# A fused attention and mixture-of-experts kernel: scaling moved to ScalarE, one gather moved ahead, seven products for layer 1 of the last expert, smaller buffers

## The chip, the cores and the metric

One NeuronCore of a Trainium2 chip runs the whole program. The metric is the time of one execution on the device in microseconds (us), as the median of the runs; smaller is better. The engines are called TensorE (PE in the profile, its weight loads PEld), VectorE (DVE), ScalarE (ACT), GpSimd (POOL) and SyncE (SP). SP issues most of the DMA transfers.

## The reference

The first stage is causal attention in a window of 128 tokens with a distance bias per head. Its output, 4608 tokens x 512, is the input x of a mixture of eight experts whose gates P are balanced by eight rounds of row and column normalisation.

```python
def _attn_ref(q, k, v):                      # q, k, v: 8 x 8 x 576 x 64
    scores = scale * np.matmul(q, k.transpose(0, 1, 3, 2))
    ...
    scores = np.where(mask, scores + bias[None], -1000000000.0)
    ...
    return np.matmul(attn, v).astype(np.float32)

def _moe_ref(x, w_gate, w1, w2):             # N, D, E, F = 4608, 512, 8, 1024
    logits = x @ w_gate
    logits = logits - logits.max()
    P = np.exp(logits)
    for _ in range(8):
        P /= P.sum(1, keepdims=True) + 1e-09
        P /= P.sum(0, keepdims=True) + 1e-09
        P *= N / E
    out = np.zeros((N, D), dtype=np.float32)
    for e in range(E):
        h = np.maximum(x @ w1[e], 0.0)
        ye = h @ w2[e]
        out += P[:, e:e + 1] * ye
    return out.astype(np.float32)
```

## The kernel before

The order of each engine's work is the order in which the program issues it; nothing reorders it. The program has two stages.

In the first stage (up to about 341 us) attention is computed, and the experts 0 and 1 of the mixture are woven into it as filler, by a planner (`Filler`) that knows the cost of each piece. Their outputs, not yet scaled by the gates, go to memory (`ysp`), as does x (`xd`). Between the stages the gates P are computed (L814 to L852).

The second stage, which the change touches, computes the experts 2 to 7. The tokens stand in 18 groups of 256 (two blocks, m = 0 and 1, of 128). A unit is one group and one expert; there are 108 units, group by group, experts 2 to 7 within each. Iteration n of the main loop (L1094) does layer 1 of unit n and layer 2 of unit n-1, with their matmuls interleaved on TensorE.

Since a gate is positive, it may be applied to x before layer 1. So each unit scales its tokens by its expert's gate: `scale_x` (L883, two instructions of 128x512 on VectorE, L889, from the token tile `xtok` to a tile `xs`), and `turn_xs` (L897) transposes the two into `xset[n % 2]` with two DMA transposes that SP issues (L901). Scaling and transposing are done two units ahead. There are four `xs` tiles, two for each parity of n. After the scaling for expert 7, `load_x` fetches the next group's tokens into `xtok`.

Layer 1 has two forms. The plain one (`l1_bank`, L939) does four banks of eight matmuls with 256 moving columns, and ACT applies the relu to each bank (L957). The other form, used from unit 6 on for all experts but 7 (`strassen(n)`, L876), is the product of 2x2 blocked matrices in seven block products in place of eight. It needs four sums of the blocks of W1 (`quads_w1`, L917, once per expert, on VectorE, L929), four sums of the blocks of x (`sums_x`, L909, three instructions on VectorE, L913 to L915), and combines the products while they accumulate in three PSUM banks pa, pb and pc: ACT copies a bank into another so that two results can grow from a common part (L1114, L1123), puts one part into SBUF (`s5s`, L1118, alternating between two halves by n), and VectorE adds that part to pb and pc (L1128, L1132). Each product is `part` (L963): eight matmuls with 128 moving columns. ACT applies the relus (L981): slots 0, 3, 1 and 2 of `h[n]`, in this order. The order of a unit is written out by hand (L1108 to L1142): a11, s1, s2, a12, s3, s4, a22 name the W1 operands of the seven products in the order of issue.

Layer 2 is in the seven product form for all units. `make_sums` (L983) forms the sums of h on VectorE (L985 to L987), the first thing in the iteration after. `product(n-1, m)` (L996, L1005) accumulates product m in one half of a PSUM bank, over all the six experts of a group; the group's first expert starts it afresh. When a group ends, `gather` (L1028, L1047) adds the products to `acc` on VectorE: products 3, 4, 5 and 2 in the next group's first unit (expert 2), 6, 7 and 1 in its second (expert 3). In that second unit products 6 and 7 are gathered right after `make_sums`, the scaling follows, then the sums out of PSUM L1128 and L1132, and product 1 is gathered behind them (L1135). Then `finish` (L1049) writes `acc` out, and `load_y` (L1014) brings the group's outputs of experts 0 and 1 back; `begin` (L1018) adds them, scaled by their gates, to `acc`: block 0 in the unit of expert 5, block 1 in that of expert 6 (two VectorE instructions each, L1020 and L1023).

The tiles come from pools of tags with a fixed number of buffers: "xT" (4: two `xset`, `acc`, `y`), "yo" (6: four `xs` and two `xtok`), "xTt" (1: `s5s`), "pmm" (4 PSUM banks: pa, pb, pc of the running unit and the one after). A tile that reuses a buffer waits for the readers of the tile before. In the last group, layer 2 of expert 7 is not done in seven products but plainly (`plain`, L1061), behind the loop.

Of the kernel before, what the change touches and what calls it, by code (L numbers as in the profile page):

```python
# [9 lines left out]
FP16 = mybir.dt.float16  # L10
FP32 = mybir.dt.float32
# [3 lines left out]
def kernel(  # L15
# [10 lines left out]
    nc = tc.nc  # L26
    AF = mybir.ActivationFunctionType
    ALU = mybir.AluOpType
# [3 lines left out]
    HD = H * Dh  # L32
# [3 lines left out]
    P = 128  # L36
# [192 lines left out]
    if True:  # L229
# [642 lines left out]
        y = per.tile([P, 2, 2, HD], FP16, name="y", tag="xT", bufs=4)  # L872
        xtok = [acc.rearrange("p m d -> p (m d)").bitcast(FP16)[:, HD * i : HD * i + HD] for i in range(2)]
        xs = [xset[i // 2][:, 4 + 2 * (i % 2) : 6 + 2 * (i % 2), :].rearrange("p q n -> p (q n)") for i in range(4)]

        def strassen(n):  # L876
            return n >= E - 2 and units[n][1] < E - 1

        def load_x(g):
            for m in range(2):  # L880
# [2 lines left out]
        def scale_x(n):  # L883
            if n >= N:
                return
            g, e = units[n]
            for m in range(2):
                blk = 2 * g + m
                nc.vector.tensor_scalar(  # L889
                    out=xs[2 * (n % 2) + m], in0=xtok[m], scalar1=P_sb[:, blk, e : e + 1], scalar2=None, op0=ALU.mult  # L890
                )
# [70 lines left out]

        def part(n, ps, w, x, start=False):  # L963

            e = units[n][1]
            for j in range(NF2):
                for k in range(2):
                    nc.tensor.matmul(  # L968
                        out=ps[:, j, :],
                        lhsT=SL[e][w][:, k, P * j : P * j + P],  # L970
                        rhs=xset[n % 2][:, x, P * k : P * k + P],
                        start=(start and j == 0 and k == 0),
                        stop=(k == 1),
                        skip_group_check=True,
                    )
# [4 lines left out]
        def relu(n, slot, src):  # L980
            nc.scalar.activation(out=h[n][:, slot], in_=src, func=AF.Relu)  # L981
# [36 lines left out]
        def begin(g, m):  # L1018
            blk = 2 * g + m
            nc.vector.tensor_scalar(  # L1020
                out=acc[:, m, :], in0=y[:, 0, m, :], scalar1=P_sb[:, blk, 0:1], scalar2=None, op0=ALU.mult
            )
            nc.vector.scalar_tensor_tensor(  # L1023
                out=acc[:, m, :], in0=y[:, 1, m, :], scalar=P_sb[:, blk, 1:2], in1=acc[:, m, :],
                op0=ALU.mult, op1=ALU.add,
            )

        def gather(g, *which):  # L1028
            q4 = acc.rearrange("p m (c n) -> p (m c) n", c=2)
# [57 lines left out]
        load_last(E - 1)  # L1087
        w2f = per.tile([P, 4, NF2, HB], FP16, name="w2f", tag="w1t", bufs=2)
        todo += sums_of(6, F1_6, w2f[:, 2], w2f[:, 3]) + sums_of(7, aux[:, 0], w2f[:, 0], w2f[:, 1])
        s5s = per.tile([P, 2, NF2, P], FP32, name="s5s", tag="xTt", bufs=1)  # L1090
        turn_xs(1)
        xs[:] = [per.tile([P, HD], FP16, name=f"xs_{i}", tag="yo", bufs=YO) for i in range(4)]
        late: tuple = ()
        for n in range(N):  # L1094
            g = units[n - 1][0]
# [2 lines left out]
            if n > 0:  # L1098
                make_sums(n - 1)
            some((4, 1, 0, 3, 2)[n] if n < 5 else 0)  # L1100
            if 0 < n <= E - 3:
                quads_w1(units[n - 1][1])
            if done:
                gather(units[n - 2][0], 6, 7)
            scale_x(n + 2)
            if n > 0 and units[n - 1][1] in (4, 5):
                begin(g, units[n - 1][1] - 4)
            if strassen(n):  # L1108
                new_h(n)
                s5 = s5s[:, n % 2]  # L1110
# [17 lines left out]
                nc.vector.tensor_tensor(out=h[n][:, 3], in0=pb, in1=s5, op=ALU.add)  # L1128
                relu(n, 3, h[n][:, 3])
                part(n, pc, "s4", B22)  # L1130
                turn_xs(n + 2)
                nc.vector.tensor_tensor(out=h[n][:, 1], in0=pc, in1=s5, op=ALU.add)  # L1132
                relu(n, 1, h[n][:, 1])
                if done:
                    gather(units[n - 2][0], 1)  # L1135
                sums_x(n + 1)
                if end:
                    gather(g, 5, 2)
                product(n - 1, 6, 7)
                part(n, pb, "a22", T4)  # L1140
                relu(n, 2, pb)
                product(n - 1, 1)  # L1142
            else:
                if done:
                    gather(units[n - 2][0], 1)
                pairs = ((3, 4), (5, 2), (6, 7), (1,))
                for i in range(4):
                    l1_bank(n, i)
                    product(n - 1, *pairs[i])
                    if end and i in (0, 1):  # L1150
                        gather(g, *pairs[i])
                turn_xs(n + 2)
                sums_x(n + 1)
            if done:
                finish(units[n - 2][0])
            if n > 0 and units[n - 1][1] == 2:
                load_y(g)
            if end:
                late = (6, 7, 1)
            if n == N - E + 2:  # L1160
# [35 lines left out]
```

## Time and profile before

| | us |
|---|---|
| median of 3 runs | 1036.04 |
| lowest and highest of them | 1035.68, 1041.56 |
| profiled execution, its own time | 1037.82 |
| its span, first to last instruction | 1034.8 |
| busy within the span: PE, PEld | 1008.6, 803.6 |
| busy within the span: DVE, ACT, POOL | 765.8, 566.8, 80.4 |
| first stage | 0 to about 341 |
| first group of the second stage (units 0 to 5) | about 341 to 380 |
| mean granted TensorE clock | 0.998 of full |

How to read the lines: a line of the timeline gives the start, the duration, the engine, the line of the program, the operation, output<-inputs, the shape of one instruction and how many were merged ("x8"); in brackets stands how long the engine idled before it and for what. A group of instructions gives count, busy time and the mean of one. A wait "A <- B: 8.0, 17, 0.6" says that A waited for B 8.0 us in all, 17 times, 0.6 us at the longest. Consecutive instructions of one engine overlap a little, so the start to start distance, and not the duration, tells what one more of them costs.

### The profile page before, as it was taken

The page shows a single profiled execution, that of the slowest core. Times are in us where ns is not written, and L with a number is a line of the kernel's source. Part 1 is how long each engine was busy: PE and PEld are TensorE (multiplying, and loading weights), DVE is VectorE, ACT ScalarE, POOL GpSimd, SP SyncE. Part 2 cuts the span into 40 slices and gives each one's busy share as a digit, 9 for nine tenths or more (in the row PEclk, how much of TensorE's full clock was granted, in tenths as well). Part 3 has the DMA queues.
Part 4 walks back from the last instruction along what each step waited for, and adds up shares of the span by engine and source line. Part 5 has one row for each costly group of instructions (what it writes and reads, how often), then busy time and mean ns, then how long its engine had stood idle before and what let it go on. Part 6 is the DMA issues. An engine that isn't in the chain of part 4 may idle for free.

```text
span 1034.8 us, 26710 instructions
## 1 busy us (share of the span) xinstructions
PE 1008.6 (97%) x11079; PEld 803.6 (78%) x11079; DVE 765.8 (74%) x1720; ACT 566.8 (55%) x973; POOL 80.4 (8%) x143
## 2 busy tenths in 40 slices
PE   7999999999999999999999999999999999999998
PEld 5645444444544789999999999999999999999997
DVE  5735666656587698778777877877877877877876
ACT  6646554555333345555555555655655655655654
POOL 1313032315110000000000000000000000000000
PEclk9999999999999999999999999999999999999999
DMA  9997799889997323324423423424433432432461
GB/s 245 203 259 174 152 224 232 204 187 186 226 186 146 88 56 93 83 52 93 84 52 93 95 45 89 103 43 87 99 57 78 94 71 64 98 76 59 97 119 37
DMA packets 264427, 122.38 MB, mean 118 GB/s; under 512 B 201969, under 2 KB 255729, under 8 KB 264305
## 3 DMA queue, kind: packets, MB, share of 16 engines
q1 hardware_dynamic: 249568, 102.68, 43.4%
q0 software_dynamic: 14304, 17.84, 10.4%
q8 instruction: 86, 1.41, 0.6%
q14 instruction: 37, 0.29, 0.1%
q10 hardware_dynamic: 432, 0.16, 0.1%
HBM read 78.30 MB, written 23.59 MB: 98 GB/s over the span
## 4 chain that ended last, share of the span: by engine, by line
PE 66%; DVE 14%; issue 2%; DMA 0%; SPq 0%; ACT 0%; DVEq 0%
PE psM L1005 25%; PE psB L968 8%; PE psy L137 7%; PE psh L115 7%; PE psh L948 7%; PE psA L968 6%; PE psC L968 5%; DVE acc L1047 4%; DVE hs L1132 2%; DVE hs L986 1%; DVE hs L985 1%; DVE hs L1128 1%; DVE hs L987 1%; PE psN L468 1%; DVE xset L913 1%
## 5 line engine op out<-in xcount | busy, mean ns | idle before, releaser
L1005 PEld LDWEIGHTS <-hs 128*128 128x128 f16 x2996 | 275.8, 98 | 35.0 <-issue 10.0
L1005 PE MATMUL psM<-w2l,hs 128*128 128x256 f16 x1440 | 186.6, 273 | 0.4 <-DVE hs L985 0.4
L968 PEld LDWEIGHTS <-w1l 128*128 128x128 f16 x2720 | 173.3, 98 | 4.0
L981 ACT ACTIVATE hs<-hs 128x512 f16<-128x512 f16 x170 | 104.3, 630 | 124.5 <-DVE hs L1128 124.5
L115 PE MATMUL psh<-xT,w1t 128*128 128x512 f16 (+1 forms) x608 | 139.7, 368 | 2.8 <-DVE xT L517 2.4
L127 ACT ACTIVATE hT<-psh 128x512 f16<-128x512 f32 (+1 forms) x144 | 83.5, 586 | 103.8 <-PE psh L115 103.3
L1005 PE MATMUL psM<-more,hs 128*128 128x256 f16 x864 | 128.9, 272 | 8.0 <-DVE acc L1047 8.0
L137 PE MATMUL psy<-w2t,hT 128*128 128x512 f16 x576 | 134.3, 379 | 0.0
L985 DVE TENSOR_TENSOR hs<-hs 128x1024 f16<-128x1024 f16 x107 | 73.8, 690 | 80.4 <-ACT hs L957 53.6
L968 PEld LDWEIGHTS <-s 128*128 128x128 f16 x1632 | 108.3, 98 | 4.6
L957 ACT ACTIVATE hs<-psh 128x512 f16<-128x512 f32 x92 | 55.0, 597 | 98.9 <-PE psh L948 96.6
L968 PE MATMUL psA<-xset,w1l 128*128 128x128 f16 x1360 | 103.7, 219 | 0.0
L137 PEld LDWEIGHTS <-hT 128*128 128x128 f16 x576 | 53.5, 98 | 60.9 <-issue 1.5
L555 DVE CAST yo<-psy 128x512 f16<-128x512 f32 x68 | 46.9, 690 | 69.8 <-PE psy L137 61.8
L115 PEld LDWEIGHTS <-w1t 128*128 128x128 f16 x608 | 54.7, 98 | 54.2 <-issue 6.3
L1128 DVE TENSOR_TENSOR hs<-psB,s5s 128x512 f16<-128x512 f32 x85 | 58.7, 690 | 41.8 <-PE psB L968 41.7
L430 ACT ACTIVATE pt<-psS 128x1024 f16<-128x1024 f32 (+2 forms) x80 | 67.7, 851 | 31.7 <-PE psS L412 24.5
L968 PE MATMUL psB<-xset,s 128*128 128x128 f16 x1088 | 82.9, 219 | 0.0
L1047 DVE TENSOR_TENSOR acc<-acc,psM 128x256 f32<-128x256 f32 (+1 forms) x162 | 73.9, 502 | 1.1 <-PE psM L1005 1.1
L948 PE MATMUL psh<-xset,w1t 128*128 128x256 f16 x576 | 74.6, 273 | 0.0
L443 DVE TENSOR_TENSOR pt<-pt,mask 128x1024 f16<-128x1024 f16 (+2 forms) x80 | 50.4, 630 | 32.0 <-ACT pt L430 31.9
L986 DVE TENSOR_TENSOR hs<-hs 128x1024 f16<-128x1024 f16 x107 | 73.2, 684 | 0.0
(113 smaller groups left out, 1386.6 us busy)
## 6 DMA issues: line engine op xcount, KB each, us to landing
y<-ysp SPq DMA_DIRECT2D x36, 256.0 KB, 3.2
ysp<-yo SPq DMA_DIRECT2D x68, 128.0 KB, 3.1
v<-in_v_dram SPq DMA_DIRECT2D x32, 256.0 KB, 4.6
out_dram<-acc SPq DMA_DIRECT2D x31, 256.0 KB, 2.6
q<-in_q_dram SPq DMA_DIRECT2D x5, 1024.0 KB, 6.6
k<-in_k_dram SPq DMA_DIRECT2D x5, 1024.0 KB, 9.2
xtok<-xd SPq DMA_DIRECT2D x34, 128.0 KB, 2.1
w2t<-in_moe_w_dram POOLq DMA_DIRECT2D x4, 1024.0 KB, 10.5
```

Of the source, the lines that this page charges most:

```text
L115: nc.tensor.matmul(out=ps[:, 0:nt], lhsT=w1ts[e][:, dt, P * ft : P * ft + P], rhs=xT[:, at : at + nb, dt, :], start=(dt == 0), stop=(dt == ...
L127: nc.scalar.activation(out=st["hT"][:, ft, 0:nt], in_=ps[:, 0:nt], func=AF.Relu)
L137: nc.tensor.matmul(out=ps, lhsT=st["hT"][:, ft, P * ms : P * ms + P], rhs=w2ts[e][:, ft, :], start=(ft == 0), stop=(ft == NFT - 1),)
L430: nc.scalar.activation(out=pt[0:nk, :, 0 : nk + nn], in_=ps[0:nk, :, :, 0 : nk + nn].rearrange("p a y n -> p (a y) n"), func=AF.Exp, scale ...
L948: nc.tensor.matmul(out=ps[:, f, :], lhsT=W1L[e][:, dt, P * ft : P * ft + P], rhs=x[:, dt], start=(f == 0 and dt == 0), stop=(dt == NDT - 1 ...
L968: nc.tensor.matmul(out=ps[:, j, :], lhsT=SL[e][w][:, k, P * j : P * j + P], rhs=xset[n % 2][:, x, P * k : P * k + P], start=(start and j = ...
L981: nc.scalar.activation(out=h[n][:, slot], in_=src, func=AF.Relu)
L985: nc.vector.tensor_tensor(out=t[:, 4:6], in0=t[:, 0:2], in1=t[:, 2:4], op=ALU.add)
L986: nc.vector.tensor_tensor(out=t[:, 6:8], in0=t[:, 1:4:2], in1=t[:, 0:3:2], op=ALU.subtract)
L1005: nc.tensor.matmul(out=Ms[bk][:, half, :], lhsT=h[n][:, LEFT[m], f, :], rhs=W2L[e][RIGHT[m]][:, f, :], start=(e == 2 and f == 0 and half = ...
L1047: nc.vector.tensor_tensor(out=a, in0=a, in1=p2, op=op)
L1128: nc.vector.tensor_tensor(out=h[n][:, 3], in0=pb, in1=s5, op=ALU.add)
```

## The change

Four things are changed in the second stage.

1. `scale_x` runs on ScalarE (`nc.scalar.mul`) in place of VectorE. In the seven product form it is issued after the relu of slot 0, in the plain form after the second bank's relu; before, it was issued ahead of the unit's matmuls.
2. In the second unit of a group, the gather of product 1 follows those of 6 and 7 directly, ahead of L1128 and L1132.
3. Layer 1 of expert 7 takes the seven product form too, from the second group on. For this `quads_w1` is called once more, in unit 6; the sum s3 of expert 7 lies in two half tiles, so it is formed in two instructions, and `part` takes a list of halves.
4. Buffers: two `xs` tiles serve both parities; `s5` and `y` share the "xTt" buffer, with one `s5` in place of two, and a `y` of one expert in place of two. So `load_y` and `begin` are called once per expert: expert 0's y is loaded in the unit of expert 3 and added to both blocks in that of expert 5, expert 1's is loaded after that and added in the unit of expert 7 (in the first group expert 0's y is added one unit later, in that of expert 6, n = 4, and expert 1's in that of expert 7, n = 5, as elsewhere).

```diff
         def strassen(n):
-            return n >= E - 2 and units[n][1] < E - 1
+            return n >= E - 2
...
             for m in range(2):
                 blk = 2 * g + m
-                nc.vector.tensor_scalar(
-                    out=xs[2 * (n % 2) + m], in0=xtok[m], scalar1=P_sb[:, blk, e : e + 1], scalar2=None, op0=ALU.mult
-                )
+                nc.scalar.mul(out=xs[2 * (n % 2) + m], in_=xtok[m], mul=P_sb[:, blk, e : e + 1])
...
+            elif e == E - 1:
+                t = per.tile([P, 2, 2, HF], FP16, name=f"s_{e}", tag="xT", bufs=4)
+                q.update(s1=t[:, 0], s2=t[:, 1])
+                q["s3"] = [per.tile([P, HF], FP16, name=f"s3_{k}", tag="yo", bufs=YO) for k in range(2)]
...
             def one(to, a, b, op):
-                nc.vector.tensor_tensor(out=q[to], in0=q[a], in1=q[b], op=op)
+                if isinstance(q[to], list):
+                    for k in range(2):
+                        nc.vector.tensor_tensor(out=q[to][k], in0=q[a][:, k], in1=q[b][:, k], op=op)
+                else:
+                    nc.vector.tensor_tensor(out=q[to], in0=q[a], in1=q[b], op=op)
...
-        def load_y(g):
-            for e in range(2):
-                nc.sync.dma_start(out=y[:, e], in_=ysp[e, 2 * g : 2 * g + 2].rearrange("m p d -> p m d"))
...
+        def load_y(g, e):
+            nc.sync.dma_start(out=y, in_=ysp[e, 2 * g : 2 * g + 2].rearrange("m p d -> p m d"))
+
+        def begin(g, e):
+            for m in range(2):
+                blk = 2 * g + m
+                if e == 0:
+                    nc.vector.tensor_scalar(
+                        out=acc[:, m, :], in0=y[:, m, :], scalar1=P_sb[:, blk, 0:1], scalar2=None, op0=ALU.mult
+                    )
+                else:
+                    nc.vector.scalar_tensor_tensor(
+                        out=acc[:, m, :], in0=y[:, m, :], scalar=P_sb[:, blk, 1:2], in1=acc[:, m, :],
+                        op0=ALU.mult, op1=ALU.add,
+                    )
...
-        s5s = per.tile([P, 2, NF2, P], FP32, name="s5s", tag="xTt", bufs=1)
+        s5y = per.tile([P, 2, GT], FP32, name="s5y", tag="xTt", bufs=1)
+        s5 = s5y[:, 0].rearrange("p (f t) -> p f t", f=NF2)
+        y = s5y[:, 1].bitcast(FP16).rearrange("p (m d) -> p m d", m=2)
         turn_xs(1)
-        xs[:] = [per.tile([P, HD], FP16, name=f"xs_{i}", tag="yo", bufs=YO) for i in range(4)]
+        xs[:] = [per.tile([P, HD], FP16, name=f"xs_{i}", tag="yo", bufs=YO) for i in range(2)] * 2
...
-            if 0 < n <= E - 3:
+            if 0 < n <= E - 2:
                 quads_w1(units[n - 1][1])
             if done:
                 gather(units[n - 2][0], 6, 7)
-            scale_x(n + 2)
-            if n > 0 and units[n - 1][1] in (4, 5):
-                begin(g, units[n - 1][1] - 4)
+                gather(units[n - 2][0], 1)
+            if n > 0 and units[n - 1][1] == 6:
+                begin(g, 1)
+            y_first_half = n > 0 and units[n - 1][1] == (5 if g == groups[0] else 4)
+            if y_first_half:
+                begin(g, 0)
...
                 part(n, pa, "a12", B21)
                 relu(n, 0, pa)
+                scale_x(n + 2)
                 product(n - 1, 5, 2)
...
                 relu(n, 1, h[n][:, 1])
-                if done:
-                    gather(units[n - 2][0], 1)
                 sums_x(n + 1)
...
-                if done:
-                    gather(units[n - 2][0], 1)
                 pairs = ((3, 4), (5, 2), (6, 7), (1,))
                 for i in range(4):
                     l1_bank(n, i)
+                    if i == 1:
+                        scale_x(n + 2)
                     product(n - 1, *pairs[i])
...
             if n > 0 and units[n - 1][1] == 2:
-                load_y(g)
+                load_y(g, 0)
+            if y_first_half:
+                load_y(g, 1)
```

More of the change, by code (lines that the diff above doesn't have):

```diff
@@ L871 @@
         acc = per.tile([P, 2, HD], FP32, name="acc", tag="xT", bufs=4)
-        y = per.tile([P, 2, 2, HD], FP16, name="y", tag="xT", bufs=4)
         xtok = [acc.rearrange("p m d -> p (m d)").bitcast(FP16)[:, HD * i : HD * i + HD] for i in range(2)]
@@ L963, in part @@
         def part(n, ps, w, x, start=False):
-            e = units[n][1]
+            q = SL[units[n][1]][w]
+            q = q if isinstance(q, list) else [q[:, k] for k in range(2)]
             for j in range(NF2):
@@ L969, in part @@
                         out=ps[:, j, :],
-                        lhsT=SL[e][w][:, k, P * j : P * j + P],
+                        lhsT=q[k][:, P * j : P * j + P],
                         rhs=xset[n % 2][:, x, P * k : P * k + P],
@@ L1012, in product @@
                     )
-        def load_y(g):
-            for e in range(2):
-                nc.sync.dma_start(out=y[:, e], in_=ysp[e, 2 * g : 2 * g + 2].rearrange("m p d -> p m d"))
[L1018 to L1026, printed above, removed]
+        def load_y(g, e):
[12 more added lines that the diff above has]
+                    )
         def gather(g, *which):
@@ L1104 @@
                 gather(units[n - 2][0], 6, 7)
-            scale_x(n + 2)
-            if n > 0 and units[n - 1][1] in (4, 5):
-                begin(g, units[n - 1][1] - 4)
+                gather(units[n - 2][0], 1)
[4 more added lines that the diff above has]
+                begin(g, 0)
             if strassen(n):
                 new_h(n)
-                s5 = s5s[:, n % 2]
                 pa = bank(n, "A")
```

## The prediction

> **What bounds the kernel now.** I read the busy times first, then the chain that ended last, then the waits, then one token group instruction by instruction.
>
> ```profile
> PE 1008.6 (97%) x11079; PEld 803.6 (78%) x11079; DVE 765.8 (74%) x1720; ACT 566.8 (55%) x973; POOL 80.4 (8%) x143
> ...
> PE 66%; DVE 14%; issue 2%; DMA 0%; SPq 0%; ACT 0%; DVEq 0%
> ```
>
> TensorE is busy throughout, so time goes only with fewer TensorE cycles or fewer TensorE waits. DVE holds 14% of the chain, so somewhere it ends last. The waits between 341 us (where the units begin) and 1030 us:
>
> ```profile
> ACT hs L981 <- DVE hs L1128: 124.5, 85, 1.8
> ...
> PE psM L1005 <- DVE acc L1047: 8.0, 17, 0.6
> ...
> PE psh L948 <- DMA xset<-xset: 1.6, 1, 1.6
> ...
> PE psM L1005 <- DVE hs L985: 0.4, 1, 0.4
> ```
>
> TensorE waits for DVE 17 times, once for each group that follows another: product 1 of a group's first expert may not overwrite its PSUM half before L1047 (gather) has read it. ACT, by contrast, idles 124.5 us in 85 units (1.46 us each) between `relu(n,0)` and `relu(n,3)`. TensorE's timeline of one group:
>
> ```profile
> 805.20 0.61 PE L968 MATMUL psA<-xset,w1l 128*128 128x128 f16 x8
> ...
> 811.56 0.60 PE L1005 MATMUL psM<-more,hs 128*128 128x256 f16 x4 [0.45 <-DVE acc L1047]
> 812.00 0.61 PE L968 MATMUL psA<-xset,w1l 128*128 128x128 f16 x8
> ...
> 818.18 0.61 PE L968 MATMUL psA<-xset,w1l 128*128 128x128 f16 x8
> ...
> 830.55 1.04 PE L948 MATMUL psh<-xset,w1t 128*128 128x256 f16 x8
> ...
> 837.10 0.61 PE L968 MATMUL psA<-xset,w1l 128*128 128x128 f16 x8
> ```
>
> Starts differ by 6.80 us (expert 3, with the wait), 6.18 (expert 4) and 6.55 (expert 7, the plain one). The same stretch on DVE and on ACT:
>
> ```profile
> 806.78 0.69 DVE L985 TENSOR_TENSOR hs<-hs 128x1024 f16<-128x1024 f16 x1
> ...
> 808.45 0.74 DVE L1047 TENSOR_TENSOR acc<-acc,psM 128x256 f32<-128x256 f32 x2
> 809.11 0.61 DVE L889 TENSOR_SCALAR xs<-xtok,L_sb 128x512 f16<-128x512 f16 x2
> 809.64 0.68 DVE L1128 TENSOR_TENSOR hs<-psB,s5s 128x512 f16<-128x512 f32 x1
> 810.24 0.68 DVE L1132 TENSOR_TENSOR hs<-psC,s5s 128x512 f16<-128x512 f32 x1
> 810.84 0.68 DVE L1047 TENSOR_TENSOR acc<-acc,psM 128x512 f32<-128x512 f32 x1
> ```
>
> ```profile
> 821.13 0.60 ACT L981 ACTIVATE hs<-psA 128x512 f16<-128x512 f32 x1
> 823.16 1.23 ACT L981 ACTIVATE hs<-hs 128x512 f16<-128x512 f16 x2 [1.42 <-DVE hs L1128]
> ```
>
> The gather of product 1 (810.84 to 811.52) is the last of an unbroken DVE row, and TensorE starts 0.04 us after it. Two scalings take 0.53 us of that row.
>
> **The change, part by part.** Times are counted from a unit's first a11 product.
>
> *Layer 1 of expert 7 in seven products.* Eight 128-wide matmuls take 0.445 us (starts 818.18 onward), so 7 x 0.445 = 3.12 us replace 4 x 0.872 = 3.49 us. The units say the same: 6.55 - 6.18 = 0.37. Seventeen units: -6.3 us. The Trainium skill, "TensorE: Matmul & The Clock Gate", Back-to-back issue gap, puts a sustained 128-wide weight load and matmul at about 81 ns; by that the seven would take 56 x 0.081 = 4.5 us and the edit would lose. The rows give 55.6 ns in 85 units, and the sum goes by them. DVE gains two sums out of PSUM and three of x in each such unit (1.2 + 1.0 us); in the six-product units the same five end in time, so I cost them at nothing. ACT swaps four evacuations for seven instructions.
>
> *Gather of product 1 moved ahead.* It now follows gathers 6 and 7, where the scalings stood. From the row above: 809.11 + 0.60 = 809.71 for L1128, 0.07 us later than now, ending at 810.39. Behind it on DVE stand L1132 and the sums of x, both of which then come earlier than now, as the gather left its place after them. TensorE's a22 product overwrites psB and waits for L1128: due at 810.50, it finds 0.05 us to spare after a hand-over of 0.06 us (as in unit 7, from 391.44 to 391.50). Relu 2 ends at about 0.76 of the next unit, and psC's s1 product, due at 0.88, needs that bank: also spare. So the wait goes whole: 16 x (6.80 - 6.18) = 9.9, and the first of the 17 was longer (unit 7 from 386.11 to 393.13, 7.02 us): 0.84. Together -10.7 us. Next latest is a22 itself; if DVE's row runs 0.2 us longer, 17 x 0.2 = 3.4 us come back, and this is the upper end. A gain beyond removal is excluded: TensorE then has no gap in the unit.
>
> *Scaling on ACT.* No row shows it. Nearest: ACT's 128x512 f16 from f16 (L981, 630 ns, paced 0.57) and, far off, the 1024-wide Exp at 851 ns; below, a copy at 570. I take 0.57 to 0.6. Between relu 0's successor at 3.46 and relu 3, due at about 4.98, lie 1.52 us, and two scalings take 1.2. Queued behind them are relus 3, 1 and 2 and the next unit's copies; those on psB and psC are what TensorE would wait for. Covered, so nothing; the cover ends at 0.76 us each, and with 0.851 about 0.05 us of each of 101 units shows, 5 us. In the six plain units of the first group they lie in ACT's 1.15 us gaps.
>
> *The scaling's transfers.* The two transposes now start after ACT, at about 4.15 and 5.4 (SP issues one in 1.19 us), the second landing 2.5 us later: 1.7 of the next unit. With one pair of xs in place of two, the next scalings (3.46 and 4.05) wait for that: 1.8 us spare. For expert 7's scaling, two token loads (about 0.4 us each on SP) go ahead of the transposes, which then land at 2.6 and leave 0.9 us. The longest landing seen is 5.7 us, so single ones will show; the upper end is 0.2 us a group, 3.4 us. On POOL nothing is moved. The y loads split into two of one expert each, both issued over a unit ahead of use in the steady state: nothing, unless they land later than 3.3 us after I expect them.
>
> *One-time cost in the second group's first unit (unit 6).* DVE runs without a break from 362 to 391 us. There the change removes two scalings a unit and adds four sums of W1 for expert 7, one of them halved: 0.6 + 0.7 + 0.7 + 0.65 = 2.65 us, ahead of the gathers. Walking it through with the rows: unit 5 no longer waits (unit 6 starts at 379.41 instead of 379.93, -0.5). DVE reaches the second `begin` at 377.6 but y's second half, issued at 375.15 behind the transposes, lands 3.2 us later at 378.35; two adds (0.68 each) end at 379.8, sums of x at 380.8, h sums at 382.4, W1 sums at 385.05, gathers 3 and 4 at 386.25, L1128 at 386.94. TensorE's a22 was due at 384.71: 2.3 us of wait, and 0.3 more in unit 7 as DVE catches up. +2.6 us. Ends: 1.8 if y is there in time, 5.1 if it lands in 5.7 us.
>
> *Start and end.* The four first scalings stand on ACT in front of L127's relus until the token load lands (about 329); those relus come 2 us later than at 328.69, and the four PSUM banks let TensorE go on: nothing, at most 0.5. In the last unit the late gathers end about 8.1 us in, when plain's first sum (7.9) is ready: nothing, at most 0.3.
>
> **Sum.** -6.3 - 10.7 - 0.5 + 2.6 = -14.9 us. The profiled execution took 1037.8 us (span 1034.8 and 3.0 around it), so it would become 1022.9; it lies 1.8 us above the median of 1036.0, which becomes 1021.1.
>
> **Rivals.** A measurement can tell about 1%, 10.4 us.
>
> A. *DVE's row or the transposes stay just too long*, and TensorE waits 0.2 to 0.45 us once or twice a group. For it: spare times of 0.05 us, landings up to 5.7 us. Against: nothing in the walk exceeds its due time. It gives back 3.4 to 7.7 us: 1024.5 to 1029.
>
> B. *The single xs pair blocks ACT.* From the point where the second transpose takes over 5.3 us to land, the second scaling ends after relu 3 was due, and every unit pays; with 5.7 throughout, about 0.4 us x 101 = 40 us come on, some 1061: slower than before. For it: 5.7 us occurs. Against: the median is 2.5. Scalings over 0.9 us each would do the same; the widest row is 0.85. The Trainium skill, "ScalarE: Activation LUTs", Rules for kernel authors, would leave a multiplication on VectorE; rows agree that DVE is quicker (347 against 630 ns), but DVE is what ends last here.
>
> C. *The seven products do not pay for expert 7.* Above 62.3 ns a matmul (3.49/56) they lose; at the 98 ns of a weight load left unhidden 56 x 0.098 = 5.5 us, 2.0 us more a unit: 1021.1 + 6.3 + 34 = 1061. Against: 55.6 ns in 85 like units. By the Trainium skill's 81 ns (the page and section named above) an estimate would be 1045; no row bears it out.
>
> D. *DVE fits y and W1's sums better than I walked it*: the one-time cost shrinks to nothing, 1018.5.
>
> **How the numbers follow.** Forecast 0.60, A 0.24, D 0.08, B 0.06, C 0.02. Time 1021.1. The range of 8 in 10 takes in D and A's bounds, from 1017.5 to 1028. Faster by over 1% (below 1025.7): forecast, D and a third of A, 0.76. Within 1%: the rest of A, 0.16. Slower: B and C, 0.08.
>
> **What would show it.** Steps right: the wait of psM for acc gone from TensorE; every later unit 6.18 us, a group 37.1 instead of 38.1; one wait of about 2 us near 385 us on psB for L1128; ACT's idle before relu 3 down from 1.4 to 0.2 us. Wrong if TensorE waits each group for L1128, for relu 2 or for ACT's copies, if scalings last over 0.76 us, or if ACT waits for transposes.

## The result and the profile after

| | before | after |
|---|---|---|
| median of 4 runs each | 1037.00 us | 1025.93 us |
| lowest to highest | 1035.68 to 1041.56 | 1023.83 to 1027.74 |
| profiled execution, its own time | 1037.82 | 1025.63 |
| its span | 1034.79 | 1023.86 |

The ratio of the times is 0.9886, with a 95% interval of 0.9854 to 0.9917: faster by 1.1%. The forecast was 1021.1 us in a range of 1017.5 to 1028.0; the gain forecast was 14.9 us, the one measured is 11.1 (10.9 in the spans of the two profiled executions).

Busy times, chain and one group of instructions, from the page of after:

```profile
PE 1000.3 (98%) x11487; PEld 801.6 (78%) x11487; DVE 749.5 (73%) x1594; ACT 722.2 (71%) x1240; POOL 78.8 (8%) x143
...
PE 74%; DVE 3%; DMA 1%; ACT 1%; issue 0%; DVEq 0%; ACTq 0%; SPq 0%
...
L888 ACT ACTIVATE xs<-xtok,L_sb 128x512 f16<-128x512 f16 x204 | 136.0, 720 | 0.6 <-DMA xset<-xs 0.6
```

DVE's share of the chain has gone from 14% to 3%, ACT's busy share from 55% to 71%, and TensorE is busy 8.3 us less: 6.4 us of it from unit 6 on (639.78 to 633.41), where expert 7's products are now 128 wide, and 1.7 us in the first stage, where TensorE's program is the same. A scaling (L888) lasts 720 ns. Two stand 0.61 us apart (820.80 below: 1.33 for the pair), close to the 0.57 to 0.6 us that the prediction took for the pace and below the 0.76 us at which the cover was to end. The waits of after between 341 us and 1030 us:

```profile
DVE hs L1141 <- ACT xs L888: 95.9, 78, 2.0
...
ACT hs L987 <- DVE hs L1141: 34.1, 97, 2.6
...
PE psB L974 <- DVE hs L1141: 2.7, 4, 1.9
```

L1141 is the former L1128, L987 the former L981, L974 the former L968, L1011 the former L1005, L1055 the former L1047. The wait of psM for the gather, 17 times before, is no longer among them. ACT's idle time in front of relu 3 went from 124.5 us to 34.1. TensorE now waits for DVE at another place, a22's product on psB, four times by this table. Its timeline shows more than the table does:

```profile
387.90 0.61 PE L974 MATMUL psB<-xset,w1l 128*128 128x128 f16 x8 [1.90 <-DVE hs L1141]
...
394.52 0.61 PE L974 MATMUL psB<-xset,w1l 128*128 128x128 f16 x8 [0.28 <-DVE hs L1141]
...
829.73 0.61 PE L974 MATMUL psA<-xset,w1l 128*128 128x128 f16 x8
...
835.91 0.61 PE L974 MATMUL psA<-xset,w1l 128*128 128x128 f16 x8
...
840.34 1.04 PE L1011 MATMUL psM<-w2l,hs 128*128 128x256 f16 x8
841.35 0.61 PE L974 MATMUL psB<-xset,w1l 128*128 128x128 f16 x8
...
842.23 0.61 PE L974 MATMUL psA<-xset,w1l 128*128 128x128 f16 x8
...
848.41 0.61 PE L974 MATMUL psA<-xset,w1l 128*128 128x128 f16 x8
```

The first two lines are the one-time cost in units 6 and 7. Below them, the unit from 829.73 and the one from 842.23 take 6.18 us, but the unit of expert 3 between them takes 6.32: its a22 starts 1.01 us after a product whose eight matmuls take 0.87 elsewhere (838.57 to 839.44), so 0.14 us late. No wait stands beside it, because the idle time is counted from a modelled end (1.04 us) that lies behind the true spacing. The reason is on DVE in the same unit:

```profile
837.50 0.69 DVE L991 TENSOR_TENSOR hs<-hs 128x1024 f16<-128x1024 f16 x1
838.10 0.68 DVE L992 TENSOR_TENSOR hs<-hs 128x1024 f16<-128x1024 f16 x1
838.81 0.42 DVE L993 TENSOR_TENSOR hs<-hs 128x512 f16<-128x512 f16 x1
839.16 1.53 DVE L1055 TENSOR_TENSOR acc<-acc,psM 128x256 f32<-128x256 f32 x3
840.61 0.68 DVE L1141 TENSOR_TENSOR hs<-psB,s5y 128x512 f16<-128x512 f32 x1
```

The three gathers (6, 7, 1) take 1.45 us from start to start of what follows. Two quarter-wide ones are 0.33 apart and a double-wide one is 0.60 long, start to start, which makes 1.26: 0.19 us are lost inside. The single starts are 839.16, 839.49 and 840.00, so they are lost in front of gather 1. L1141 starts 4.70 us after the unit's first a11 product; the prediction walked it to 4.51. ACT's timeline in a unit of expert 6 (from 817.36), with the scaling in its new place:

```profile
820.31 0.60 ACT L987 ACTIVATE hs<-psA 128x512 f16<-128x512 f32 x1
820.80 1.33 ACT L888 ACTIVATE xs<-xtok,L_sb 128x512 f16<-128x512 f16 x2
822.33 1.23 ACT L987 ACTIVATE hs<-hs 128x512 f16<-128x512 f16 x2 [0.20 <-DVE hs L1141]
```

The pair of scalings takes 1.33 us, and 0.20 us of ACT's gap are left in front of relu 3. In the unit of expert 3, where L1141 comes later, 0.65 us are left.

### The profile page after: what moved, and what is told of

Same layout as the page of the kernel before. It is cut to its first block, busy times and chain, and to the rows that moved or that the text cites. A ratio compares the mean times of both kernels' runs of the same rounds, so it can differ in the third digit from the quotient of the medians.

```text
span 1023.9 us, 27787 instructions
## 1 busy us (share of the span) xinstructions
PE 1000.3 (98%) x11487; PEld 801.6 (78%) x11487; DVE 749.5 (73%) x1594; ACT 722.2 (71%) x1240; POOL 78.8 (8%) x143
## 4 chain that ended last, share of the span: by engine, by line
PE 74%; DVE 3%; DMA 1%; ACT 1%; issue 0%; DVEq 0%; ACTq 0%; SPq 0%
PE psM L1011 30%; PE psB L974 13%; PE psA L974 9%; PE psC L974 9%; PE psy L137 5%; PE psh L115 5%; PE psh L953 2%; DVE acc L1055 1%; PE psN L468 1%; DMA acc<-xd 0%; DVE hs L1141 0%; PE psS L412 0%; DVE hs L991 0%; DVE hs L992 0%; DMA s5y<-ysp 0%
## 5 line engine op out<-in xcount | busy, mean ns | idle before, releaser
L1011 PEld LDWEIGHTS <-hs 128*128 128x128 f16 x2996 | 271.7, 98 | 22.4
L1011 PE MATMUL psM<-w2l,hs 128*128 128x256 f16 x1440 | 186.6, 273 | 0.0
L974 PEld LDWEIGHTS <-w1l 128*128 128x128 f16 x2720 | 173.2, 98 | 8.9 <-issue 3.0
L127 ACT ACTIVATE hT<-psh 128x512 f16<-128x512 f32 (+1 forms) x144 | 83.3, 586 | 100.9 <-PE psh L115 100.2
L987 ACT ACTIVATE hs<-hs 128x512 f16<-128x512 f16 x204 | 125.0, 630 | 34.3 <-DVE hs L1141 34.1
L1141 DVE TENSOR_TENSOR hs<-psB,s5y 128x512 f16<-128x512 f32 x102 | 70.4, 690 | 103.7 <-ACT xs L888 95.9
L974 PEld LDWEIGHTS <-s 128*128 128x128 f16 x2040 | 135.3, 98 | 5.8
L888 ACT ACTIVATE xs<-xtok,L_sb 128x512 f16<-128x512 f16 x204 | 136.0, 720 | 0.6 <-DMA xset<-xs 0.6
L1011 PE MATMUL psM<-more,hs 128*128 128x256 f16 x864 | 129.0, 273 | 0.0
L974 PE MATMUL psA<-xset,w1l 128*128 128x128 f16 x1360 | 103.7, 219 | 0.0
L974 PE MATMUL psB<-xset,s 128*128 128x128 f16 x1360 | 103.7, 219 | 0.0
L991 DVE TENSOR_TENSOR hs<-hs 128x1024 f16<-128x1024 f16 x107 | 74.0, 691 | 23.5 <-ACT hs L987 16.8
L1135 ACT COPY psC<-psB 128x512 f32<-128x512 f32 x102 | 58.1, 570 | 36.5 <-PE psB L974 36.5
L1130 ACT COPY s5y<-psC 128x512 f32<-128x512 f32 x102 | 59.8, 586 | 25.5 <-PE psC L974 25.5
L1055 DVE TENSOR_TENSOR acc<-acc,psM 128x256 f32<-128x256 f32 (+1 forms) x162 | 74.1, 503 | 2.1
## 6 DMA issues: line engine op xcount, KB each, us to landing
w2t<-in_moe_w_dram POOLq DMA_DIRECT2D x4, 1024.0 KB, 10.9
```

What stands on the lines that cost most here:

```text
L127: nc.scalar.activation(out=st["hT"][:, ft, 0:nt], in_=ps[:, 0:nt], func=AF.Relu)
L888: nc.scalar.mul(out=xs[2 * (n % 2) + m], in_=xtok[m], mul=P_sb[:, blk, e : e + 1])
L974: nc.tensor.matmul(out=ps[:, j, :], lhsT=q[k][:, P * j : P * j + P], rhs=xset[n % 2][:, x, P * k : P * k + P], start=(start and j == 0 and ...
L991: nc.vector.tensor_tensor(out=t[:, 4:6], in0=t[:, 0:2], in1=t[:, 2:4], op=ALU.add)
L1011: nc.tensor.matmul(out=Ms[bk][:, half, :], lhsT=h[n][:, LEFT[m], f, :], rhs=W2L[e][RIGHT[m]][:, f, :], start=(e == 2 and f == 0 and half = ...
L1055: nc.vector.tensor_tensor(out=a, in0=a, in1=p2, op=op)
```

## Where the time went

Both traces cut at the same instructions (us):

| stretch | before | after | change |
|---|---|---|---|
| up to the first unit | 341.44 | 342.56 | +1.12 |
| units 0 to 5 | 38.49 | 37.97 | -0.52 |
| units 6 and 7 | 13.19 | 14.86 | +1.67 |
| expert 3, second unit of 16 groups | 6.80 each, the last 6.97 | 6.32 each, the last 6.62 | -7.6 |
| expert 7, 17 units | 6.55 each | 6.18 each, the last 6.54 | -5.9 |
| rest of the units | | | +0.1 |
| from `plain` to the end | 7.12 | 7.27 | +0.15 |

The first row holds 0.56 us of scatter (the two programs are alike up to about 326 us, and the same matmul starts at 317.64 and 318.20) and 0.56 us in the hand-over from the first stage to the units, 23.80 against 24.36 us.

## The experiments

What was to be told apart: the missing 2.3 us of expert 3's units. Theory 1 is that gather 1, standing directly behind gather 7 whose quarter of `acc` it reads, pays for that dependence, and L1141 behind it comes late for a22. Theory 2, its rival, is what the table of waits names: L1141 waits for ACT's scaling (95.9 us, 78 times). For the one-time cost the rivals are the W1 sums of expert 7 and the late y. The rest tests what each part is worth, and how much room is left. Every kernel is the changed one with the edit shown. Ratios stand against the kernel before on the same chip; since the first stage, alike in all, begins the units anywhere from 338.6 to 345.5 us, the edits are compared by two stretches of the profiles:

| kernel | first unit at | units 6 on, to `plain` | ratio to before, 95% interval |
|---|---|---|---|
| before | 341.44 | 647.74 | |
| after | 342.56 | 636.05 | 0.9886 [0.9854, 0.9917] |
| e1, scaling on VectorE | 343.51 | 647.19 | 0.9972 [0.9955, 0.9988] |
| e2, gather 1 back | 345.45 | 641.01 | 0.9943 [0.9921, 0.9964] |
| e3, expert 7 plain | 341.08 | 639.55 | 0.9906 [0.9883, 0.9929] |
| e4, gathers woven in | 343.65 | 633.23 | 0.9861 [0.9834, 0.9887] |
| e5, W1 sums later | 343.23 | 633.32 | 0.9862 [0.9842, 0.9881] |
| e6, one scaling twice | 343.82 | 641.52 | 0.9932 [0.9911, 0.9954] |
| e8, e6 with three xs | 340.37 | 637.47 | 0.9880 [0.9865, 0.9895] |
| e9, three xs alone | 338.60 | 635.59 | 0.9856 [0.9830, 0.9882] |
| e7, e4 and e5 and first scalings on VectorE | 340.58 | 631.26 | 0.9835 [0.9813, 0.9857] |

Units 0 to 5 took 37.97 or 37.98 us in every changed kernel, so a difference of a few tenths in the second stage can be read from one profile.

### e1_scale_on_vector: the scaling back on VectorE, at its new place

```diff
-                nc.scalar.mul(out=xs[2 * (n % 2) + m], in_=xtok[m], mul=P_sb[:, blk, e : e + 1])
+                nc.vector.tensor_scalar(
+                    out=xs[2 * (n % 2) + m], in0=xtok[m], scalar1=P_sb[:, blk, e : e + 1], scalar2=None, op0=ALU.mult
+                )
```

> The changed kernel with the scaling of x alone put back on VectorE, at the place in the order where ScalarE has it now (in the seven product units it so stands right ahead of the sums out of PSUM). Theory 1 (VectorE's row sets the second unit of a group, ScalarE is covered): the two scalings, paced 0.53 us together in the trace of before, lengthen that unit from 6.32 to about 6.85 us in each of 17 groups and the second group's first unit by 0.5; all other units stay at 6.18, because VectorE has 0.6 to 2.0 us idle there. 9.5 us slower than the changed kernel, about 1035. Theory 2 (VectorE's sum out of PSUM is released by ScalarE's scaling, as the table of waits says with 95.9 us in 78 units): the sum starts earlier than 4.25 us after the unit's start once ScalarE does not scale, and time is gained where it was the last to come, so no slower, 1026 or less.

Measured: 1035.45 us (10 runs), and 11.1 us more in the stretch than after. Expert 3's units take 6.84 us as expected. Unit 6 takes 10.98, 2.74 us more than in after, where 0.5 was expected. Part of that is TensorE's clock: behind a wait of 2.71 us for L1143 (to 390.81) the granted clock is 0.50 until 393.96, 128-wide matmuls stand 107 ns apart in place of 55.6, and about 1.6 us are lost by it. In the units of the other experts, unit 6 apart, nothing changed: they take 6.18 us in both kernels (the last group's last 6.54), and L1141 starts 4.25 us behind the unit's start in both kernels (829.73 to 833.98 in after, 839.52 to 843.77 here). The table of waits of this kernel names another releaser for the same start:

```profile
ACT hs L989 <- DVE hs L1143: 164.3, 102, 4.6
DVE hs L1143 <- PE psB L976: 51.6, 65, 2.0
```

So TensorE's s3 product releases L1141 (here L1143); ACT was named in after because it signals last of several that had to be there. The rival falls: with the 95.9 us of "waits for ACT" gone, no unit became shorter, and in expert 3's units of after DVE was not idle in front of L1141 at all. The Trainium skill, "ScalarE: Activation LUTs", Rules for kernel authors, tells to use VectorE for a multiplication. Here it speaks against the change, and the measurement decides the other way: on VectorE, the engine that ends last in these units, the same multiplications cost 11.1 us more.

### e2_gather_back: gather 1 behind L1145 again

```diff
-                gather(units[n - 2][0], 1)
...
+                if done:
+                    gather(units[n - 2][0], 1)
```

> The changed kernel with the gather of product 1 alone put back behind the sums out of PSUM; the scaling stays on ScalarE. Theory 1: VectorE then reaches the first sum by about 4.1 us and the gather ends at 6.14 us into the unit, where TensorE wanted the bank at 5.74: the unit of expert 3 takes 6.6 us in place of 6.32, TensorE waits for acc again, 17 x 0.3 = 5 us slower than the changed kernel, about 1031. Rival (the scaling's leave from VectorE alone removed the wait, and the moved gather did nothing or harm): 6.18 us units, up to 2 us faster than the changed kernel.

Measured: 1032.53 us (9 runs), 5.0 us more in the stretch; expert 3's units take 6.62 us, sixteen times. TensorE waits for the gather again, here in its timeline:

```profile
848.41 0.60 PE L1011 MATMUL psM<-more,hs 128*128 128x256 f16 x4 [0.28 <-DVE acc L1055]
```

With e1 this prices both parts of the change on the same unit: gather moved alone 6.84, scaling moved alone 6.62, both 6.32, neither (before) 6.80 us. Moving the gather alone gains nothing, because the first sum out of PSUM then starts 5.23 us into the unit in place of 4.44, late by what the gather costs there; moving the scaling alone gains 0.18 us, and both together 0.48.

### e3_plain_e7: expert 7's layer 1 in four products again

```diff
-            return n >= E - 2
+            return n >= E - 2 and units[n][1] < E - 1
...
-            if 0 < n <= E - 2:
+            if 0 < n <= E - 3:
```

> The changed kernel with expert 7's layer 1 alone back in the plain form, with no sums of its W1. Theory 1: its units take 6.55 us in place of 6.18 in 16 groups (the last group's gained nothing), +5.9 us, and the wait in the second group's first unit (8.24 us) falls to none, -2.5 us: 3.4 us slower than the changed kernel, about 1029. Rival (128 column matmuls cost more than they save, about 81 ns each): 17 us faster than the changed kernel, about 1009.

Measured: 1028.56 us; 3.5 us more in the stretch, 0.4 less behind it. Expert 7's units take 6.55 us again (-5.9 lost), but units 6 and 7 take 6.18 and 6.32, as the sums of W1 are gone. Both parts are as expected. The rival by which 128-wide products cost more than they save falls here.

### e4_woven: gathers between the sums, never two dependent neighbours

```diff
-        def make_sums(n):
+        def make_sums(n, old=None):
...
+            if old is not None:
+                gather(old, 6, 7)
...
+            if old is not None:
+                gather(old, 1)
...
-            if done:
-                gather(units[n - 2][0], 6, 7)
-                gather(units[n - 2][0], 1)
```

The first insertion stands behind the first of the three sums, the second ahead of the last.

> The changed kernel with the gathers woven into the sums of h, in the second unit of a group: sum 4 and 5, gathers 6 and 7, sum 6 and 7, gather 1, sum 1. No instruction is added or left out. Theory 1a (gather 1 waits about 0.19 us for gather 7's result, which it reads directly behind it, as the last sum of h waits 0.11 us for the one before): with another instruction between each such pair VectorE reaches the sum out of PSUM 0.3 us earlier, TensorE's a22 finds it done, and the unit of expert 3 takes 6.18 us in place of 6.32: 16 x 0.135 + 0.3 = 2.4 us faster than the changed kernel, about 1023.5. Theory 2 (the 0.135 us come from ScalarE, whose scaling is the last to release that sum): 6.32 us as now, no difference.

Measured: 1022.99 us; 2.8 us less in the stretch, and 99 of its units take 6.18 us. DVE in the unit that starts at 835.18:

```profile
836.76 0.68 DVE L991 TENSOR_TENSOR hs<-hs 128x1024 f16<-128x1024 f16 x1
837.37 0.74 DVE L1059 TENSOR_TENSOR acc<-acc,psM 128x256 f32<-128x256 f32 x2
838.03 0.68 DVE L994 TENSOR_TENSOR hs<-hs 128x1024 f16<-128x1024 f16 x1
838.63 0.68 DVE L1059 TENSOR_TENSOR acc<-acc,psM 128x512 f32<-128x512 f32 x1
839.23 0.42 DVE L997 TENSOR_TENSOR hs<-hs 128x512 f16<-128x512 f16 x1
839.56 0.68 DVE L1142 TENSOR_TENSOR hs<-psB,s5y 128x512 f16<-128x512 f32 x1
```

The same six instructions take 2.80 us from the start of L991 to that of L1142; in after they take 3.11 (837.50 to 840.61). Only the order differs, so the 0.31 us is the price of neighbours that depend on each other: 0.19 at the gathers, the rest at the sums (838.10 to 838.81 is 0.71 where 0.60 is usual; the last sum does not read the result of the one before, it overwrites a slot that the one before reads). L1142 stands 4.38 us behind the unit's start. The theory holds.

### e5_sums_later: the W1 sums of expert 7 in units 8 and 10

```diff
-            if 0 < n <= E - 2:
+            if 0 < n <= E - 3:
...
+            if n in (E, E + 2):
+                quads_w1(E - 1, (n - E) // 2)
```

`quads_w1` is split behind its first two sums.

> The changed kernel with the five sums of expert 7's W1 moved out of the second group's first unit: two of them (three instructions) to that group's third unit, two to its fifth, where VectorE is idle for 1.65 and 1.96 us; they are wanted in its sixth. Theory 1 (they alone make the one-time cost): units of 8.24 and 6.62 us become 6.18 and 6.32, 2.4 us faster than the changed kernel, about 1023.5. Rival (y's second half, which lands late in the unit before, holds VectorE back): of the 2.4 us at most 1 is gained.

Measured: 1024.27 us; 2.7 us less in the stretch, units 6 and 7 take 6.18 and 6.31 us. The one-time cost (2.06 us in unit 6, 0.30 in unit 7) was the W1 sums, whole; the y that lands late costs nothing once they are elsewhere. The remaining 0.3 us lie in the last group's unit of expert 3, which takes 6.32 us here and 6.62 in after; the account of the prediction comes back to it.

### e6_scale_twice: the first scaling of each pair done twice, from unit 8 on

```diff
-                nc.scalar.mul(out=xs[2 * (n % 2) + m], in_=xtok[m], mul=P_sb[:, blk, e : e + 1])
+                for _ in range(2 - m if n >= E else 1):
+                    nc.scalar.mul(out=xs[2 * (n % 2) + m], in_=xtok[m], mul=P_sb[:, blk, e : e + 1])
```

> The changed kernel with the first of a unit's two scalings done twice from the third group's start on and a little before (unit 8), so that ScalarE has one more instruction of 0.72 us (paced about 0.61) per unit. Theory 1 (the cover ends 0.20 us after the second scaling, and 0.13 us more lie before psC's bank is wanted): relu 3 comes 0.41 us late, about 0.3 us of it reaches TensorE in each unit but the second of a group, where the sum comes later anyway: some 80 x 0.3 = 24 us slower, about 1050. Rival (ScalarE still has room, its busy share is 71%): no difference.

Measured: 1031.38 us; 5.5 us more in the stretch where 24 was expected. A miss. Nearly all units still take 6.18 and 6.32 us, although ACT is no longer idle in front of relu 3. In a unit of expert 6 relu 3 starts 5.43 us in, 0.45 late, but relu 2, the last of the queue behind it, ends at 0.87 us of the next unit in place of 0.51, and TensorE wants its bank at 0.88. So the room behind ACT's 0.20 us was 0.37 us there, and not the 0.13 that I had taken (the walk of expert 3's unit has 0.12).

The 5.5 us lie in a few units: 1.3 in units 6 and 7 (8.75 and 7.41 us), 1.1 in three of 6.4 to 6.7 us, and 3.0 in unit 104, around 995 us (9.20). In units 6 and 7 it is TensorE's clock again:

```profile
389.24 0.65 PE L975 MATMUL psB<-xset,w1l 128*128 128x128 f16 x8 [1.98 <-DVE hs L1142]
...
390.54 1.06 PE L975 MATMUL psA<-xset,w1l 128*128 128x128 f16 x8
...
393.54 0.61 PE L975 MATMUL psB<-xset,s 128*128 128x128 f16 x8
```

Behind the wait of 1.98 us the granted clock is 0.50 from 389.7 to 393.0, and matmuls take twice their time. In after the same wait is 1.90 us long and in e2 1.95, and the clock stays at 1.00. ACT in unit 104:

```profile
991.53 0.60 ACT L988 ACTIVATE hs<-psA 128x512 f16<-128x512 f32 x1
992.02 1.48 ACT L889 ACTIVATE xs<-xtok,L_sb 128x512 f16<-128x512 f16 x2
997.21 0.72 ACT L889 ACTIVATE xs<-xtok,L_sb 128x512 f16<-128x512 f16 x1 [3.72 <-DMA xset<-xs]
```

The second scaling waits 3.72 us for a transpose that reads the tile it is to overwrite, and relus stand behind it. In this kernel transposes took up to 8.6 us from issue to landing (in after up to 5.2, median 2.5). In the three units of 6.4 to 6.7 us ACT had waited 0.5 to 0.8 us for a transpose in the unit before.

### e8_twice_three_xs and e9_three_xs: a third xs tile, with and without the doubled scaling

```diff
-    XPE, YO, XSB = 3, 6, 12
+    XPE, YO, XSB = 3, 7, 12
...
-                nc.scalar.mul(out=xs[2 * (n % 2) + m], in_=xtok[m], mul=P_sb[:, blk, e : e + 1])
+                nc.scalar.mul(out=xs[(2 * n + m) % 6], in_=xtok[m], mul=P_sb[:, blk, e : e + 1])
...
-        xs[:] = [per.tile([P, HD], FP16, name=f"xs_{i}", tag="yo", bufs=YO) for i in range(2)] * 2
+        xs[:] = [per.tile([P, HD], FP16, name=f"xs_{i}", tag="yo", bufs=YO) for i in range(3)] * 2
```

`turn_xs` reads the tiles by the same index. In e8 the scaling is doubled as in e6.

> The kernel with the first scaling done twice, with three tiles for the scaled x used in turn in place of one pair, so that each is written again one and a half units later and not one (one buffer more in its pool). With one pair it took 641.5 us from the second group's first unit to the last plain layer, 5.5 us more than the changed kernel's 636.05, though nearly all units kept 6.18 or 6.32 us: the loss lay in a few units where ScalarE waited for transposes. Theory A (the single pair: a transpose that lands late now blocks ScalarE, which has no room to catch up): with three tiles these waits go, and the stretch takes about 637 to 638 us. Theory B (it is the added work itself): 641.5 as before.

> The changed kernel with the same three tiles for the scaled x in turn, and nothing else. Theory A says that the single pair costs the changed kernel next to nothing, because ScalarE still has about 0.55 us of room per unit: its one wait of 0.6 us goes, the stretch takes 636.0 us, within 0.3. If the smaller buffers cost more than that, it takes 635 or less.

Measured: e8 1024.84 us, 4.05 us less in the stretch than e6; e9 1021.14 us, 0.46 less in the stretch than after, just below the range that was expected (the rest of e9's distance to after is the first stage, 4 us shorter in that profile, and no merit of the edit).

With three tiles ACT's waits for transposes are gone, which returns 1.1 us in three units and 1.2 in unit 104. There 1.8 us stay (8.01 us): a transpose lands 8.4 us after its issue, and the sums of x wait 2.6 us for it (2.3 in e6), whatever the number of tiles. Another 1.3 us came back in units 6 and 7, where TensorE waited 1.87 us and its clock did not fall. So rival B's mechanism is there and made up 2.3 of e6's 5.5 us. In the changed kernel it costs nothing that can be seen: ACT's one wait for a tile (0.6 us, in unit 94) lengthened no unit, and 0.36 of e9's 0.46 us lie in units 102 and 103, which e5, with one pair, ran as fast.

### e7_all: woven gathers, later sums, and the first four scalings on VectorE

The edits of e4 and e5, and:

```diff
-                nc.scalar.mul(out=xs[2 * (n % 2) + m], in_=xtok[m], mul=P_sb[:, blk, e : e + 1])
+                if n < 2:
+                    nc.vector.tensor_scalar(
+                        out=xs[2 * (n % 2) + m], in0=xtok[m], scalar1=P_sb[:, blk, e : e + 1], scalar2=None, op0=ALU.mult
+                    )
+                else:
+                    nc.scalar.mul(out=xs[2 * (n % 2) + m], in_=xtok[m], mul=P_sb[:, blk, e : e + 1])
```

> Both of these together, and the first four scalings, before the units begin, on VectorE again (ScalarE's hold-up of L127's relus made TensorE wait 0.4 us). If the three add up: 2.4 + 2.4 + 0.5 = 5.3 us faster than the changed kernel, about 1020.6, with every unit from the second group on at 6.18 us but the last group's. If one shadows another, less.

Measured: 1020.06 us (1018.64 to 1025.48), and 4.8 us less in the stretch than after, as expected. The hand-over takes 23.80 us, but e2, e5 and e9 reach that with ScalarE's scalings too, so the third edit is not shown to be worth anything. It is the version with the lowest ratio, 0.9835, and the shortest stretch. The busy times in the stretch from unit 6 to `plain` follow for three kernels (window, its length, then busy time and count of PE, PEld, DVE, ACT, POOL, the granted clock, the DMA share, GB/s). First the kernel before:

```profile
379.93:1027.67 647.74, 639.78 (x8162) 599.04 (x8160) 517.54 (x1161) 376.69 (x664) 0.88 (x1) 1.00 0.37 78
```

The same stretch of the changed kernel:

```profile
380.53:1016.59 636.06, 633.41 (x8571) 598.30 (x8569) 503.11 (x1047) 522.83 (x914) 0.87 (x1) 1.00 0.37 80
```

And of e7_all:

```profile
378.55:1009.80 631.25, 631.05 (x8570) 598.36 (x8568) 500.19 (x1047) 524.12 (x914) 0.87 (x1) 1.00 0.38 81
```

The length less PE's busy time is 7.96, 2.65 and 0.20 us. PE's ends are modelled and hide small delays: four units of e7_all still take 0.05 to 0.36 us more than 6.18 (the last 6.54). Hardly more than that is left to take out of this stretch by ending waits.

## Why the prediction came out as it did

**The step that failed** is "809.11 + 0.60 = 809.71 for L1128 ... it finds 0.05 us to spare". Its size was wrong by 0.19 us, more than the spare time: gather 1 was costed at its own 0.60 us behind gather 7, and by the move it got a neighbour on which it depends. So the term "16 x (6.80 - 6.18) = 9.9" measured 7.6: 0.48 in fifteen units and 0.35 in the last. The last is no part of the mechanism: in the unit ahead of it (102) L1141 starts 4.60 us in, in place of 4.25, behind an idle DVE, and DVE's work stays 0.3 us late through the next; e5 and e9, where it starts at 4.25, ran that unit in 6.32 and 6.31. Single units with this 0.35 us stand in most kernels, before among them; what causes it is open. The mechanism, 0.14 us a group, is rival A in a smaller form than I gave it (0.2 to 0.45): 0.05 us of spare time, over a row walked with durations to two decimals, was no ground for "the wait goes whole". e4 shows the cause by taking the neighbours apart. So one of the signs that the prediction named as wrong came, TensorE late for L1141 in each group (a group takes 37.22 us, not 37.1), beside those that it named as right: the wait near 385 us (1.90 us, to 387.90) and ACT's 0.20 us.

**Expert 7**: forecast -6.3, measured -5.9. Sixteen units gained 0.37 us as worked out. The last one, already crowded on DVE by the last group's adds and gathers, gained nothing: the sums out of PSUM that were costed at nothing start 0.7 us late there.

**Units 0 to 5**: forecast -0.5, measured -0.52. **Units 6 and 7**: forecast +2.6 for the one-time cost less 0.84 for the wait of the first group, +1.76; measured +1.67: a one-time cost of 2.36 and a unit 7 that shrinks by 0.69 without it, as it too has the late L1141. e5 confirms that the W1 sums are the cause, so rival D, by which they would fit in, did not come.

**Scaling on ACT**: the time was that of the forecast, nothing, and so nearly was the pace, 0.61 us. A single scaling lasts 0.72 us where the nearest row, a relu without a scale from a tile, lasts 0.63; no run tests whether the scale makes the difference. The bound at 0.76 held. One row was misread: 851 ns is the mean of three shapes of Exp, and the 1024-wide one took 1026 ns, so "the widest row is 0.85" does not hold and the far bound on ACT was set too low. The Trainium skill, "ScalarE: Activation LUTs", What ACT_TABLE_LOAD costs, gives 186 ns, 93 ns more for each operand by pointer and 0.833 ns an element; that makes an estimate of 706 ns for 512 elements, and the trace agrees within 3% (706 to 724 ns, median 722).

**The transfers**: forecast nothing, at most 3.4; measured nothing that can be seen (e9). **Start and end**: nothing, at most 0.5 and 0.3; measured 0.56 and 0.15. Of the 0.56, 0.40 us stand in the trace as TensorE's wait for an L127 relu, behind the four scalings. In e2, e5 and e9, with the same scalings in the same place, the hand-over took 23.80 us as before, so this cost does not come in every execution.

By the spans 4.0 us of gain are missing (14.9 against 10.9): 2.3 of expert 3, 0.4 of expert 7, and 1.3 of start and end, of which 0.56 is the scatter of the first stage. By the medians it is 3.8 (14.9 against 11.1); the time lies 4.8 us above the forecast, as the median of before came out 1 us higher with its fourth run.

**The chances**: the time lies at 1025.9, on the border of "faster by over 1%" (0.76) and "within 1%" (0.16); by ratio it is faster by 1.1%, and its interval reaches 0.8%. B and C had 0.08 together. C was not near (e3). B was nearer than its price told: e6 shows that with one scaling more on ACT a single late transpose can cost 3 us in a unit.

## What to carry to other kernels

When an instruction is moved, look at its new neighbours as well as its duration: if it depends on the instruction in front of it, price the pair from a pair in the trace that depends likewise, and put an independent instruction between them. An engine's spare time is counted unit by unit, and ending a wait in one unit may need two moves at once (here 0.48 us together, 0.18 and nothing alone). A releaser in a table of waits is only a candidate: compare the start of the waiting instruction with and without the supposed cause.

## What the runs showed of the hardware

- A DVE instruction directly behind one that it depends on started later than an independent one: by 0.19 us for gather 1 behind gather 7 (839.49 to 840.00 in after, where independent neighbours of 0.41 us stand 0.33 apart), by 0.19 for the last sum of W1, which reads the one before (384.57 to 385.36, usually 0.60), and by 0.11 for the last sum of h. One independent instruction between removed it (e4). The Trainium skill, "VectorE: DVE Perf Modes", The DRAIN you can't avoid, reports eight copies that took the same time with and without a semaphore after each, as the pipe empties after every instruction anyway. These traces add that a neighbour that depends on the one before comes later than one that does not.
- After a wait of TensorE of 1.98 us (e6) or 2.71 us (e1) the granted clock was 0.50 for about 3.2 us, and 128-wide matmuls stood 107 ns apart. After waits of 1.86 to 1.95 us in the same place (after, e2, e4, e8, e9) it stayed at 1.00. Whether the length alone decides was not tried.
- Eight 128-wide weight loads and matmuls took 0.445 us (55.6 ns each) also in the 17 units that are new in this form.
- A transpose of a 128x512 tile landed 2.5 us after its issue at the median, and 5.2 us at the longest in after; with the scaling done twice the longest took 8.6 (e6) and 8.4 us (e8). What made these late was not tried.
- The first stage, whose TensorE program is the same in all kernels, took between 338.6 and 345.5 us up to the first unit. The profile with the lowest start had a mean granted clock of 1.000, the one with the highest 0.996; whether the clock is the whole cause was not tried.
